# One ordered instruction region, four weighting buffers, paired weight sums, and SBUF pools moved to multiples of 512 bytes, in a fused linear-attention and expert kernel

## The chip, the cores and the metric

The kernel runs on one core of a Trainium2 chip. The metric is the device time of one execution in microseconds (us); lower is better. The granted clock of TensorE (PE) is given as a share of its full 2.4 GHz.

## The reference

Three stages follow each other; all data is float32.

```python
# 1: linear attention with a decaying state, batch 2, 8 heads, 768 steps, head size 48
cur = einsum('bhd,bhe->bhde', u * k_t, v_t)
y_t = einsum('bhd,bhde->bhe', r_t, state + cur)
state = w_t[..., None] * state + einsum('bhd,bhe->bhde', k_t, v_t)
# 2: x is y as 1536 tokens x 384; w_in 384 x 2048, w_out 2048 x 384
h = x @ w_in
x = where(h > 0, h, exp(min(h, 0)) - 1) @ w_out
# 3: four experts, w1[e] 384 x 1024, w2[e] 1024 x 384; p are normalised domain_probs
for e in range(4):
    out += p[:, e:e+1] * (maximum(x @ w1[e], 0) @ w2[e])
```

## The kernel before

Every 128x128 by 128x512 product is done in float32r with both operands split into a high and a low part: three matmuls (`PASSES`: high x high, high x low, low x high) accumulate in one PSUM bank. Splitting costs a copy on ScalarE (ACT) for the high part and a subtraction on VectorE (DVE) or GpSimd (POOL) for the low part, of weights and of activations alike.

The work runs in this order. The attention works on 12 chunks of 128 steps. The feed-forward stage has 48 steps (`step`): `h` multiplies tokens with `w_in` (L355, 9 matmuls), `e` and `el` make the activation and its low part, `z` multiplies with `w_out` (L375, 9 matmuls), `dr` adds a finished block into `x2` and splits it again. Its weights come in 32 pieces (`wl` load, `wa`, `wb`, `wc` convert). A hand-written list, `ORDER`, gives the sequence of attention and feed-forward tokens. A `|` in it (its place is `cut`) marks where the attention's memory is given up. What lies in front of it is one ordered region, what follows is a second one.

The expert stage (`experts`) is a third ordered region. It makes a list of events, each with a key, and issues them in order of key. The keys count the groups of three matmuls on PE: `row` has 36 groups `plain` (the first product of two units, L553), then `product` (L525) and `second` (L575) in turn, about five to six. The first product of the other 14 units is done for blocks of 2x3 weights and 3x3 tokens at once by a scheme of 15 products instead of 18. For it, sums of weight blocks are made on POOL (`sum_blocks`, L444, 11 of 128x128 for each unit, list `SUMS`) and sums of tokens on DVE (`TOKENS`, L505). `taken` (L537) adds the finished products into `terms` on DVE, `hidden_hi` (L565) and `hidden_lo` (L568) apply the maximum and split, `second` is the product with `w2`. After it `weighted` (L584, DVE) multiplies by the token's share into a `scaled` buffer, and `added` (L589, POOL) adds that to `x2`. `shares` (L478 to L486) makes the shares from `dp`, `load_share` spreads them. `load_blocks` (L440) and `load_second` (L462) load weights from the queue of SyncE (SP).

Events with negative keys belong in front of the first matmul of the stage: `shares` has -200, the loads of the first units have -95, -85 and -39, the weight sums of the first summed unit lie between -14 and -2.

Two regions are ordered each within itself. How the instructions of the third region stand between those of the second is decided when the program is built, not by the keys.

On-chip memory (SBUF) is handed out to pools from both ends, tile after tile, padded to 32 bytes. From the left, 2,176 bytes are taken (a 2,048-byte scratch area and four padded constants), then the pool `const` takes 704 bytes, then come `x` (49,152 bytes), `x2`, and the pools of the second and third stage, all in sizes that are multiples of 512. So each tile from `x` on begins 320 bytes past a multiple of 512: `x`, `w` of the feed-forward stage, `hl`, `w2s`. From the right, the top is 229,344; `xb` takes 12,288 bytes there and the others (`blocks`, `sums`, `raw2`) follow in multiples of 512, so each begins 480 bytes past one. The weights of `plain` and `product` are `sums` (480), those of `second` are `w2s` (320); the tokens that they stream are `x` (320), `xb` (480) and `hl` (320).

Of the kernel before, what the change touches and what calls it, by code (L numbers as in the profile page):

```python
# [9 lines left out]
F32 = mybir.dt.float32  # L10
F32R = mybir.dt.float32r
# [3 lines left out]
ALU = mybir.AluOpType  # L15
PSUM = bass.MemoryType.PSUM

P = 128
C = 128
NCH = 12  # L20
# [10 lines left out]
PASSES = ((0, 0), (0, 1), (1, 0))  # L31
WARM = 3
TERMS = 18

# [10 lines left out]
LOADED = [(0, 0), (1, 0), (0, 1), (1, 2), (0, 2), (1, 1)]  # L47
W0, W3, W1, W5, W2, W4 = range(5, 11)
SLOT = {11: 0, 0: 1, 8: 2, 9: 3, 14: 4, 7: W0, 2: W3, 3: W2, 6: W4, 4: 11, 10: 12, 13: 13, 5: 14, 12: 15, 1: 16}
SUMS = [(SLOT[0], W1, "-", W4), (SLOT[13], W1, "-", W0), (SLOT[4], SLOT[13], "-", W4), (SLOT[5], W5, "-", W3),  # L50
        (SLOT[10], SLOT[5], "-", W2), (SLOT[12], SLOT[13], "-", SLOT[5]), (SLOT[1], SLOT[10], "+", W0),
        (SLOT[11], SLOT[4], "+", W3), (SLOT[9], W2, "-", W5), (SLOT[8], W5, "-", W4), (SLOT[14], W2, "-", W1)]
PLACE = dict(zip(TURNS, [9, 10, 11, 12, 13, 14, 0, 3, 6, 1, 4, 7, 2, 5, 8]))

TOKENS = [("q", (1, 1), (2, 1)), (0, "q", (0, 1)), (6, (1, 2), None), (3, (2, 2), None), (4, 0, (1, 2)), (7, 4, (0, 2)),
# [5 lines left out]
ORDER = """  # L61
# [27 lines left out]
def kernel_body(ctx, tc, wkr, vv, uu, w_in, w_out, w1, w2, dp, out):  # L89
    nc = tc.nc  # L90
    const = ctx.enter_context(tc.tile_pool(name="const", bufs=1))
# [3 lines left out]
    pools = {}  # L95
# [9 lines left out]
    m1 = ExitStack()  # L105
# [11 lines left out]
    warm = bank()  # L117
    for _ in range(WARM):
        nc.tensor.matmul(warm, lhsT=first1[:, 0:P], rhs=first1[:, 0:512], start=True, stop=True)
    ones = const.tile([P, 1], F32, name="ones")  # L120
    nc.gpsimd.memset(ones, 1.0)
    ident = const.tile([P, P], F32, name="ident")
    make_identity(nc, ident)
# [271 lines left out]
    def do(order):  # L395
        for token in order:
            name, n, e = re.fullmatch(r"([a-z]+)(\d+)([ADMPS]?)", token).groups()
            kind = step if name in ("h", "e", "el", "z", "dr") else piece if name in ("wl", "wa", "wb", "wc") else attn
            if (kind, n) not in work:
                work[kind, n] = kind(int(n))  # L400
            work[kind, n][name](*e)

    cut = ORDER.index("|")
# [6 lines left out]
    def early_pools(es):  # L410
        for name, bufs in (("xb", 1), ("blocks", 2), ("sums", 3), ("raw2", 2)):
            pools[name] = es.enter_context(tc.tile_pool(name=name, bufs=bufs, side="right"))

    def late_pools(es):
        for name, bufs in (("w2", 2), ("terms", TERMS), ("hl", 4), ("shares", 4), ("scaled", 2), ("guard", 1)):
            pools[name] = es.enter_context(tc.tile_pool(name=name, bufs=bufs))
        for name, bufs in (("chain", 5), ("second", 3)):
            pools[name] = es.enter_context(tc.tile_pool(name=name, bufs=bufs, space=PSUM))
        pools["rows"] = es.enter_context(tc.tile_pool(name="rows", bufs=1, space=bass.MemoryType.DRAM))

    def experts(guard=False):

        events = []

        def at(key, run, *args):
            events.append((key, len(events), run, args))

        xb = pools["xb"].tile([P, 3, 2, 512], F32R, name="xb")
        pairs = x.rearrange("q k (b n) s c -> q (k b) (n s c)", b=3)

        def tokens(r):
# [4 lines left out]
        blocks, split = {}, {}  # L436

        def load_blocks(u):
            blocks[u] = pools["blocks"].tile([P, 17, P], F32, tag="blocks", name="blocks")
            nc.sync.dma_start(blocks[u][:, 5:11].rearrange("q b c -> q (b c)"), w1[:, u])  # L440

        def sum_blocks(u, r, a, op, c):
            t = blocks[u]
            nc.gpsimd.tensor_tensor(t[:, r], t[:, a], t[:, c], ALU.subtract if op == "-" else ALU.add)  # L444

        def split_hi(u, part, first, n, i, m):
            if i == 0:
# [27 lines left out]
        rows = pools["rows"].tile([4, NT], F32, name="rows")  # L475
        prs = {}

        def shares():  # L478
            t = pools["raw2"].tile([P, 768], F32, tag="raw2", name="share")
            share, total = t[:NCH, 0:512].rearrange("n (e c) -> n e c", e=4), t[:NCH, 512:640]  # L480
            nc.sync.dma_start(share, dp)
            nc.vector.tensor_reduce(total, share.rearrange("n e c -> n c e"), mybir.AxisListType.X, ALU.add)
            nc.vector.tensor_scalar_add(total, total, 1e-9)
            nc.vector.reciprocal(total, total)
            nc.vector.tensor_tensor(share, share, total.unsqueeze(1).to_broadcast([NCH, 4, C]), ALU.mult)
            nc.sync.dma_start(rows.rearrange("e (n c) -> n e c", n=NCH), share)  # L486
# [74 lines left out]
        hls, sums = {}, {}  # L561
# [7 lines left out]

        def second(h, b, f, d):  # L570
            if f == 0:
                sums[d] = pools["second"].tile([P, 512], F32, tag="second", name="second")
            w = w2s[h].rearrange("p s (f d) -> p s f d", f=4)
            for i, (sa, sm) in enumerate(PASSES):
                nc.tensor.matmul(sums[d], lhsT=w[:, sa, f, d * P:(d + 1) * P], rhs=hls[4 * h + f, b][:, sm],  # L575
                                 start=f == i == 0, stop=f == 3 and i == 2)

        scaled = {}
# [29 lines left out]
            nc.vector.tensor_reduce(flag, n, mybir.AxisListType.X, ALU.max)  # L608


        seconds = [(h, b, f, d) for h in range(8) for b in range(3) for f in range(4) for d in range(3)]
        row = [("plain", f, b, j) for b in range(3) for f in range(4) for j in range(3)]
        done = 0
# [6 lines left out]
        place = {g: n for n, g in enumerate(row)}  # L620
        for n, (kind, *g) in enumerate(row):
# [5 lines left out]
            elif kind == "second":  # L627
# [4 lines left out]
                if f == 3:  # L632
                    at(n + 0.6, weighted, *g[:2], d)
                    if h:
                        at(n + 0.8, added, *g[:2], d)
        at(-200, shares)
        for e in range(4):
            for b in range(3):
                at(place["second", 2 * e, b, 0, 0] - 60, load_share, e, b)
        for u in range(16):  # L640
            n = place["product", u, 0] if u > 1 else -20 + 10 * u
            at(n - 75, load_blocks, u)
            if u < 2:
                for i in (0, 3):
                    at(n - 20 + i, split_hi, u, 0, 5, 6, i, 3)
                    at(n - 19 + i, split_lo, u, 0, 5, 6, i, 3)
                continue
            for i, s in enumerate(SUMS):
                at(n - 50 + 1.2 * i, sum_blocks, u, *s)
            for part, first, size, k in ((0, 9, 8, n - 34), (1, 0, 7, n - 14)):  # L650
                for i in (0, 4):
                    at(k + i, split_hi, u, part, first, size, i, min(4, size - i))
                    at(k + i + 1.4, split_lo, u, part, first, size, i, min(4, size - i))
        for h in range(8):
            n = place["second", h, 0, 0, 0]
            for m in range(2):
                at(n - 70 + m, load_second, h, m)
                for q in range(2):
                    at(n - 38 + 6 * m + 3 * q, second_hi, h, m, q)
                    at(n - 37 + 6 * m + 3 * q, second_lo, h, m, q)  # L660
        for i, t in enumerate(TOKENS):
            at(1.2 + 1.1 * i, sum_tokens, *t)
        for i, r in enumerate(TURNS):
# [14 lines left out]

    early, late = ExitStack(), ExitStack()
    early_pools(early)  # L680
    with tc.manual_schedule():
        do(ORDER[cut + 1:])
    m1.close()
    late_pools(late)
    experts(guard=True)
    late.close()
    early.close()

# [112 lines left out]
```

## Time and profile before

| | us |
|---|---|
| median of 3 runs | 698.1 (695.83 to 701.0) |
| the profiled execution | 697.27 |
| its span, first to last instruction | 695.5 |
| PE busy in the span | 652.5 |
| DVE, POOL, ACT busy | 493.0, 413.6, 305.6 |

Busy time of PE includes the tail of each matmul, which overlaps the next one; so PE's speed is read from the distance between the starts of two matmuls (the pitch), and from idle time in front of one.

### The profile page before, as it was taken

Reading aid. Unit: us, or ns where it says so; the run is one execution under the profiler, and the core shown is the slowest. Engines: PE = TensorE matmul, PEld = TensorE weight load, DVE = VectorE, ACT = ScalarE, POOL = GpSimd, SP = SyncE. Lnnn points to the kernel's source line nnn. Section 1 sums busy time; section 2 is a strip of 40 time slices with the busy share of each in tenths; the row PEclk is TensorE's granted clock in tenths of the full one; section 3 lists DMA queues with packets and bytes.
Section 4 is the critical chain, followed back from the end, with each engine's and each line's share of the span. In section 5 each row is a group of like instructions: output and inputs, shape, how many; then the busy total and the mean of one; then the engine's idle time right before and its main releaser. Section 6 shows DMA issues by size and latency. Waiting matters only on the chain.

```text
span 695.5 us, 9183 instructions
## 1 busy us (share of the span) xinstructions
PE 652.5 (94%) x3314; PEld 521.1 (75%) x3314; DVE 493.0 (71%) x686; ACT 305.6 (44%) x584; POOL 413.6 (59%) x415
## 2 busy tenths in 40 slices
PE   6778999889999999999999999999999999999994
PEld 4666778668888888786888868778688688788773
DVE  7989997728563642798675777876867777777764
ACT  2343645637565663648343524433443335233220
POOL 5898684565332451659643865876876777644241
PEclk9989999999999999999999999999999999999998
DMA  7655552322202100011102121021120122200012
GB/s 264 206 180 182 180 186 62 115 89 82 83 24 68 47 24 1 3 65 50 57 17 74 63 60 54 23 85 31 42 94 15 39 68 69 76 0 1 0 46 96
DMA packets 20971, 50.83 MB, mean 73 GB/s; under 512 B 2680, under 2 KB 3880, under 8 KB 20916
## 3 DMA queue, kind: packets, MB, share of 16 engines
q1 hardware_dynamic: 20772, 50.15, 23.1%
q8 instruction: 28, 0.46, 0.3%
q14 instruction: 27, 0.22, 0.1%
q10 hardware_dynamic: 144, 0.00, 0.0%
HBM read 46.58 MB, written 2.38 MB: 70 GB/s over the span
## 4 chain that ended last, share of the span: by engine, by line
PE 68%; DVE 12%; POOL 11%; issue 6%; DMA 2%; ACT 1%; SPq 0%; DVEq 0%; POOLq 0%; ACTq 0%
PE second L575 25%; PE bank L375 11%; PE bank L355 9%; PE chain_a L525 8%; PE chain_b L525 4%; PE chain_c L525 3%; PE chain_d L525 3%; DVE terms L505 2%; DVE hl L568 2%; DVE scaled L584 2%; POOL x L589 2%; POOL rd L141 2%; POOL kr L141 1%; PE chain_e L525 1%; POOL hl L144 1%
## 5 line engine op out<-in xcount | busy, mean ns | idle before, releaser
L575 PE MATMUL second<-hl,w2s 128*128 128x512 f32 x864 | 237.0, 396 | 2.7 <-DVE scaled L584 1.4
L575 PEld LDWEIGHTS second<-hl,w2s 128*128 128x128 f32 x864 | 161.8, 188 | 43.6 <-DVE scaled L584 3.6
L589 POOL TENSOR_TENSOR x<-scaled,x 128x512 f32<-128x512 f32 x60 | 81.3, 1375 | 96.3 <-DVE scaled L584 96.3
L375 PE MATMUL bank<-hl,w 128*128 128x512 f32 x432 | 106.1, 396 | 4.4 <-POOL hl L144 4.2
L355 PE MATMUL bank<-x,w 128*128 128x512 f32 x432 | 104.0, 392 | 0.2 <-DVE e L363 0.2
L144 POOL TENSOR_TENSOR sums<-blocks,sums 128x512 fp32r<-128x512 f32 (+1 forms) x60 | 79.4, 1331 | 37.5 <-ACT sums L148 34.2
L375 PEld LDWEIGHTS bank<-hl,w 128*128 128x128 f32 x432 | 81.2, 190 | 23.2 <-POOL hl L144 5.2
L568 DVE SCALAR_TENSOR_TENSOR hl<-terms,hl 128x512 fp32r<-128x512 f32 x96 | 90.2, 943 | 7.1 <-ACT hl L565 6.8
L355 PEld LDWEIGHTS bank<-x,w 128*128 128x128 f32 x432 | 80.9, 188 | 18.0 <-DVE e L363 0.6
L444 POOL TENSOR_TENSOR blocks<-blocks 128x128 f32<-128x128 f32 x154 | 86.1, 583 | 1.2
L525 PE MATMUL chain_a<-x,sums 128*128 128x512 f32 x210 | 61.2, 399 | 6.4 <-DVE terms L537 6.3
L363 DVE SCALAR_TENSOR_TENSOR e<-e,bank 128x512 f32<-128x512 f32 x48 | 32.4, 681 | 47.6 <-ACT e L359 43.3
L565 ACT ACTIVATE hl<-terms 128x512 fp32r<-128x512 f32 x96 | 58.1, 623 | 16.4 <-PE second L575 11.5
L144 POOL TENSOR_TENSOR hl<-e,hl 128x512 fp32r<-128x512 f32 x26 | 35.2, 1358 | 49.4 <-ACT hl L148 48.8
L537 DVE TENSOR_TENSOR terms<-terms,chain_a 128x512 f32<-128x512 f32 x42 | 28.7, 684 | 42.2 <-PE chain_a L525 42.2
L148 ACT ACTIVATE sums<-blocks 128x512 fp32r<-128x512 f32 (+1 forms) x60 | 35.6, 595 | 49.7 <-PE chain_b L525 30.2
L148 ACT ACTIVATE terms<-chain_b 128x512 f32<-128x512 f32 x28 | 16.8, 600 | 88.7 <-PE chain_b L525 88.7
L525 PEld LDWEIGHTS chain_a<-x,sums 128*128 128x128 f32 x210 | 39.1, 188 | 18.0 <-DVE terms L537 9.0
L584 DVE TENSOR_TENSOR scaled<-second,pr 128x512 f32<-128x512 f32 x63 | 43.1, 685 | 13.3 <-PE second L575 8.5
L148 ACT ACTIVATE hl<-e 128x512 fp32r<-128x512 f32 x48 | 30.1, 629 | 34.3 <-PE bank L375 23.9
L358 ACT ACTIVATE e<-bank 128x512 f32<-128x512 f32 x48 | 28.5, 593 | 33.0 <-POOL hl L144 15.6
L148 ACT ACTIVATE terms<-chain_a 128x512 f32<-128x512 f32 x28 | 16.7, 598 | 50.4 <-PE chain_a L525 50.4
(116 smaller groups left out, 998.2 us busy)
## 6 DMA issues: line engine op xcount, KB each, us to landing
kr<-in_wkr SPq DMA_DIRECT2D x12, 512.0 KB, 3.9
raw<-in_w_in SPq DMA_DIRECT2D x16, 384.0 KB, 3.4
raw<-in_w_out SPq DMA_DIRECT2D x16, 384.0 KB, 3.3
blocks<-in_w SPq DMA_DIRECT2D x16, 384.0 KB, 3.4
raw<-in_w SPq DMA_DIRECT2D x16, 384.0 KB, 4.5
v<-in_vv SPq DMA_DIRECT2D x12, 456.0 KB, 4.4
w<-in_wkr SPq DMA_DIRECT2D x12, 258.5 KB, 4.0
gw<-in_wkr SPq DMA_DIRECT2D x12, 258.0 KB, 2.9
```

The lines of the kernel that those rows point to most:

```text
L144: engines[e].tensor_tensor(o, a, b.bitcast(F32), ALU.subtract)
L148: nc.scalar.activation(out=o, in_=a, func=AF.Copy)
L355: nc.tensor.matmul(ph, lhsT=wi[:, sa, f, kk, :], rhs=x[:, kk, c0:c0 + nch, sm], start=(kk == 0 and i == 0), stop=(kk == 2 and i == 2))
L363: nc.vector.scalar_tensor_tensor(b["e"], b["e"], -1.0, b["ph"], ALU.add, ALU.max)
L375: nc.tensor.matmul(pxs[q, bl][d], lhsT=wo[:, sa, f, d * P:(d + 1) * P], rhs=b["t"][:, sm], start=(f == 0 and i == 0), stop=(f == 3 and i = ...
L444: nc.gpsimd.tensor_tensor(t[:, r], t[:, a], t[:, c], ALU.subtract if op == "-" else ALU.add)
L525: nc.tensor.matmul(banks[c], lhsT=weights(u, r, sa), rhs=tokens(r)[:, sm], start=r in HEADS and i == 0, stop=i == 2, skip_group_check=True)
L565: nc.scalar.activation(out=hls[f, b][:, 0], in_=results[f, b], func=AF.Relu)
L568: nc.vector.scalar_tensor_tensor(hls[f, b][:, 1], results[f, b], 0.0, hls[f, b][:, 0].bitcast(F32), ALU.max, ALU.subtract)
L575: nc.tensor.matmul(sums[d], lhsT=w[:, sa, f, d * P:(d + 1) * P], rhs=hls[4 * h + f, b][:, sm], start=f == i == 0, stop=f == 3 and i == 2)
L584: nc.vector.tensor_tensor(o, sums[d], prs[h // 2, b], ALU.mult)
L589: (nc.vector if last else nc.gpsimd).tensor_tensor(x2[:, d, s], scaled[d], x2[:, d, s], ALU.add)
```

## The change

Five edits. The tokens behind `|` and the events of the expert stage become one ordered region: the tokens get negative keys, counted backwards from the end in steps of 3 for each `h` and `z` (which have 3 groups each), and `switch`, which closes the feed-forward pools and opens the late ones, is an event with key 0. So the tokens begin at about -237, the load for the shares is at -250 and their arithmetic at -100; events that need the late pools get a key of at least 0. The `scaled` pool has four buffers instead of two. Weight sums are made in pairs: six POOL instructions for a unit instead of eleven, five of them on two blocks at a time. The second products of the last half expert's middle block (h 7, b 1) accumulate in banks of the pool `chain`. And padding moves the pools: `const` becomes 896 bytes (`ones` is cut out of a 49-column tile), so the left side begins at a multiple of 512; `xb` becomes 12,768 bytes, so the right side does.

```diff
+EDGE = 120
-SUMS = [(SLOT[0], W1, "-", W4), (SLOT[13], W1, "-", W0), (SLOT[4], SLOT[13], "-", W4), (SLOT[5], W5, "-", W3),
-        (SLOT[10], SLOT[5], "-", W2), (SLOT[12], SLOT[13], "-", SLOT[5]), (SLOT[1], SLOT[10], "+", W0),
-        (SLOT[11], SLOT[4], "+", W3), (SLOT[9], W2, "-", W5), (SLOT[8], W5, "-", W4), (SLOT[14], W2, "-", W1)]
+SUMS = [((SLOT[13], SLOT[5]), (W1, W5), "-", (W0, W3)), ((SLOT[4], SLOT[12]), (SLOT[13],) * 2, "-", (W4, SLOT[5])),
+        ((SLOT[9], SLOT[10]), (W2, SLOT[5]), "-", (W5, W2)), ((SLOT[11], SLOT[1]), (SLOT[4], SLOT[10]), "+", (W3, W0)),
+        ((SLOT[0], SLOT[8]), (W1, W5), "-", (W4, W4)), ((SLOT[14],), (W2,), "-", (W1,))]
-    ones = const.tile([P, 1], F32, name="ones")
+    ones = const.tile([P, 49], F32, name="ones")[:, 0:1]
+        pools["rows"] = es.enter_context(tc.tile_pool(name="rows", bufs=1, space=bass.MemoryType.DRAM))
-        for name, bufs in (("w2", 2), ("terms", TERMS), ("hl", 4), ("shares", 4), ("scaled", 2), ("guard", 1)):
+        for name, bufs in (("w2", 2), ("terms", TERMS), ("hl", 4), ("shares", 4), ("scaled", 4), ("guard", 1)):
-        xb = pools["xb"].tile([P, 3, 2, 512], F32R, name="xb")
+        xb = pools["xb"].tile([P, 3072 + EDGE], F32R, name="xb")[:, 0:3072].rearrange("q (r s c) -> q r s c", r=3, s=2)
+        def places(t, p):
+            if p[0] == p[-1]:
+                return t[:, p[0]:p[0] + 1].to_broadcast([P, len(p), P])
+            d = p[1] - p[0]
+            return t[:, p[0]:p[1] + (1 if d > 0 else -1):d]
         def sum_blocks(u, r, a, op, c):
-            t = blocks[u]
-            nc.gpsimd.tensor_tensor(t[:, r], t[:, a], t[:, c], ALU.subtract if op == "-" else ALU.add)
+            nc.gpsimd.tensor_tensor(*(places(blocks[u], p) for p in (r, a, c)), ALU.subtract if op == "-" else ALU.add)
+        def load_shares():
+            given["t"] = pools["raw2"].tile([P, 768], F32, tag="raw2", name="share")
+            nc.sync.dma_start(given["t"][:NCH, 0:512].rearrange("n (e c) -> n e c", e=4), dp)
...
-                sums[d] = pools["second"].tile([P, 512], F32, tag="second", name="second")
+                k = "chain" if h == 7 and b == 1 else "second"
+                sums[d] = pools[k].tile([P, 512], F32, tag=k, name=k)
...
+        n, keys = 0, []
+        for token in reversed(lead):
+            n -= 3 * (token[0] in "hz")
+            keys.append(n)
+        for token, n in zip(lead, reversed(keys)):
+            at(n, do, [token])
+        if switch:
+            at(0, switch)
...
-        at(-200, shares)
+        at(-250, load_shares)
+        at(-100, shares)
-                at(place["second", 2 * e, b, 0, 0] - 60, load_share, e, b)
+                at(max(0, place["second", 2 * e, b, 0, 0] - 60), load_share, e, b)
-                at(n - 50 + 1.2 * i, sum_blocks, u, *s)
+                at(n - 50 + 2 * i, sum_blocks, u, *s)
-                    at(n - 38 + 6 * m + 3 * q, second_hi, h, m, q)
-                    at(n - 37 + 6 * m + 3 * q, second_lo, h, m, q)
+                    at(max(0, n - 38 + 6 * m + 3 * q), second_hi, h, m, q)
+                    at(max(0, n - 37 + 6 * m + 3 * q), second_lo, h, m, q)
...
-    with tc.manual_schedule():
-        do(ORDER[cut + 1:])
-    m1.close()
-    late_pools(late)
-    experts(guard=True)
+    def switch():
+        m1.close()
+        late_pools(late)
+    experts(guard=True, lead=ORDER[cut + 1:], switch=switch)
```

## Rows read from the trace of the kernel before

**Rows 1.** The page's first parts: engine busy times, and PE's granted clock by slice.
```profile
PE 652.5 (94%) x3314; PEld 521.1 (75%) x3314; DVE 493.0 (71%) x686; ACT 305.6 (44%) x584; POOL 413.6 (59%) x415
...
PEclk9989999999999999999999999999999999999998
```

**Rows 2.** Busy time by stretch; columns PE, PEld, DVE, ACT, POOL, granted clock, DMA.
```profile
118.00:293.00 175.00, 170.45 (x740) 139.15 (x739) 96.37 (x153) 99.97 (x178) 77.31 (x71) 0.99 0.19 55
...
290.00:330.00 40.00, 37.60 (x151) 28.99 (x150) 34.86 (x37) 25.16 (x48) 28.80 (x25) 0.96 0.14 48
330.00:658.00 328.00, 320.37 (x1366) 254.64 (x1364) 235.95 (x337) 122.05 (x229) 207.17 (x237) 1.00 0.15 47
658.00:696.00 38.00, 25.77 (x108) 19.32 (x107) 20.54 (x28) 5.09 (x9) 12.21 (x8) 0.92 0.17 65
```

**Rows 3.** PE in order of time in the feed-forward stage: start, length, count.
```profile
181.17 4.24 PE L355 MATMUL bank<-x,w 128*128 128x512 f32 x18
185.25 1.07 PE L375 MATMUL bank<-hl,w 128*128 128x512 f32 x4
```

**Rows 4.** The same in the plain products of the expert stage.
```profile
297.70 5.53 PE L553 MATMUL chain_p<-x,sums 128*128 128x512 f32 x23
```

**Rows 5.** The chain that ended last, 340 to 350 us: start, length, what, count.
```profile
339.84 0.70 PE chain_a L525 x3
...
349.60 0.47 PE second L575 x2
```

**Rows 6.** PE in order of time just after the first second products.
```profile
325.24 1.49 PE L575 MATMUL second<-hl,w2s 128*128 128x512 f32 x3
...
327.80 0.41 PE L575 MATMUL second<-hl,w2s 128*128 128x512 f32 x1
```

**Rows 7.** Busy time and granted clock in 325 to 327 us, columns as in group 2.
```profile
325.00:327.00 2.00, 2.00 (x7) 1.54 (x6) 1.34 (x3) 2.00 (x5) 2.00 (x3) 0.50 0.00 0
```

**Rows 8.** Busy time in 447 to 455 us, columns as in group 2.
```profile
447.00:455.00 8.00, 6.73 (x28) 4.73 (x26) 7.79 (x11) 1.30 (x3) 5.62 (x7) 1.00 0.01 3
```

**Rows 9.** POOL in order of time, 132 to 147 us.
```profile
140.10 5.18 POOL L444 TENSOR_TENSOR blocks<-blocks 128x128 f32<-128x128 f32 x11
145.24 1.26 POOL L144 TENSOR_TENSOR hl<-e,hl 128x512 fp32r<-128x512 f32 x1
```

**Rows 10.** PE in order of time, 133 to 152 us; in brackets the idle time ahead.
```profile
137.92 2.11 PE L375 MATMUL bank<-hl,w 128*128 128x512 f32 x8 [1.96 <-POOL hl L144]
...
146.55 3.49 PE L375 MATMUL bank<-hl,w 128*128 128x512 f32 x8 [2.22 <-POOL hl L144]
149.84 2.46 PE L355 MATMUL bank<-x,w 128*128 128x512 f32 x9
```

**Rows 11.** SP's queue in order of time, 118 to 140 us.
```profile
126.75 0.33 SPq L486 DMA_DIRECT2D rows<-share  x1
129.53 0.38 SPq L175 DMA_DIRECT2D raw<-in_w_out  x1
```

**Rows 12.** DVE in order of time, 448 to 456 us.
```profile
450.98 0.69 DVE L584 TENSOR_TENSOR scaled<-second,pr 128x512 f32<-128x512 f32 x1 [0.21 <-POOL x L589]
...
452.19 1.81 DVE L568 SCALAR_TENSOR_TENSOR hl<-terms,hl 128x512 fp32r<-128x512 f32 x1
```

**Rows 13.** PE's waits: for whom, us in total, times, longest.
```profile
PE chain_a L525 <- DVE terms L537: 6.3, 5, 1.3
...
PE second L575 <- DVE scaled L584: 1.4, 3, 0.8
PE chain_b L525 <- DVE terms L537: 1.3, 5, 0.3
```

**Rows 14.** POOL's groups by shape: busy us, mean ns of one, idle us ahead.
```profile
L444 POOL TENSOR_TENSOR blocks<-blocks 128x128 f32<-128x128 f32 x154 | 86.1, 583 | 1.2
...
L144 POOL TENSOR_TENSOR sums<-blocks,sums 128x384 fp32r<-128x384 f32 x18 | 20.1, 1120 | 3.2 <-DMA blocks<-in_w 3.2
L141 POOL TENSOR_TENSOR rd<-kr,a 128x512 f32<-128x512 f32 x11 | 18.0, 1633 | 5.3 <-DVE a L254 2.1 <-DVE raw L181 2.0 <-PE bank L327 1.2
```

## The prediction before the run

> **What bounds the kernel now.** I read the page's busy times first, then busy time by stretch, then PE in order of time, and last the waits. PE is busy 652.5 of 695.5 us and its granted clock is full in nearly every slice [rows 1]. From 118 to 293 us it has 170.5 of 175 busy, from 330 to 658 us 320.4 of 328 [rows 2]. There the time is the number of matmuls times their pitch, plus a few gaps. In between, from 290 to 330 us, DVE has 34.9 of 40 us and PE waits for token sums: DVE bounds that stretch [rows 2].
>
> So the pitch is the first thing to look at, and it isn't one number. In the feed-forward stage 18 matmuls start in 185.25 - 181.17 = 4.08 us, 226.7 ns each [rows 3]; a single one's record is 4.24 less 17 pitches, 0.39 us. In the plain products it is (5.53 - 0.39) / 22 = 233.6 ns [rows 4]. Where `product` and `second` take turns, 42 matmuls pass from 339.84 to 349.60, 232.4 ns each [rows 5]. All of these are matmuls of 512 columns at the full clock. Just after a gap of PE six matmuls take 327.80 - 325.24 = 2.56 us, 426.7 ns each [rows 6], and the granted clock there is 0.50, the 1.2 GHz level [rows 7]: exactly 512 columns at that clock. At 2.4 GHz the same would be 213.3. So at the full clock something other than the columns adds 13.3 ns in the feed-forward stage and 20 in the plain products, and at half the clock it is hidden.
>
> What differs between these two places is where the weights lie: 320 bytes past a multiple of 512 (`w`), 480 past it (`sums`). The streamed tokens (`x`, 320) are the same, with the same strides. 13.3 to 20 is 2 to 3, and 320 to 480 is 2 to 3 as well, also when one counts from the last multiple of 128 (64 and 96). A straight line through the two points meets zero excess at offset zero. Two points are few, but this is the reading that I bet on.
>
> **The change part by part.** The sum is made against the profiled execution's 697.3 us, 0.8 under the median of the runs.
>
> *Alignment.* No row shows a weight tile on a multiple of 512, so its pitch lies between 213.3 (the columns alone) and today's 226.7, and above that if two equal offsets get in each other's way. I take 213.3, where the line through the two rows ends. Feed-forward: 740 matmuls between 118 and 293 us [rows 2] x 13.4 ns = 9.9 us (in front of 118 the attention sets the pace, and I count nothing). From 290 to 330 us nothing, because DVE bounds it. From 330 to 658 us: 1366 matmuls [rows 2] x 19.1 ns = 26.1 us, less the spots where DVE is full, 7.79 of 8 us [rows 8], at the end of each of six half experts: 6 x 28 matmuls x 19.1 ns = 3.2 us don't count there. 22.9 us remain. In the tail 108 matmuls [rows 2], most of them at 226.7 already by the same way of counting: 108 x 13.4 = 1.5 us. Together 34.3 us.
>
> The Trainium skill (TensorE: Matmul & The Clock Gate, Back-to-back issue gap) gives N / 2.4 + 2.5 ns for the warm gap, 215.8 for 512 columns. The trace shows 226.7 at best, so this chip's kernel doesn't reach it before the change. With 215.8 as the aligned pitch the sum below would be about 5 us smaller and the time near 657.
>
> *One ordered region.* Today the work for the experts is done early, around 119 to 145 us, in front of the feed-forward work that PE needs. On POOL eleven weight sums take 5.18 us from 140.10, and the low part `hl` that PE waits for comes behind them at 145.24 [rows 9]. PE idles 1.96 us at 137.92 and 2.22 at 146.55, and after the second gap eight matmuls take 3.29 us instead of 1.81, the clock having fallen [rows 10]. On SP the store of the shares waits for DVE until 126.75, and the load of `w_out` behind it goes at 129.53 [rows 11]. After the change the shares come at -100 (some 67 us before the stage's end), the splits of the first units at -40 to -26, the sums at -14 to -4. These gaps go: 2.0 + 2.2 + 1.5 + 0.3 for the restarts = 6.0 us. The work itself doesn't go; it is put between the `e`, `el` and `z` of the late feed-forward stage, where POOL is busy for 77 of 175 us and DVE for 96 [rows 2]. The queues are in order, so each such block can hold back one `hl`: the eleven sums as six take about 5 us on POOL, in six places. The bounds are nothing and the whole 6 us again on each of the two engines, 12; I take 1.5, since the pieces are spread and the engines are half idle. On SP, the share's load now waits at the region's head for memory of the attention; behind it are the next `wl` loads. Net 4.5 us. The order behind key 0 hardly changes, so the stretch at 290 to 330 us stays as it is.
>
> *Four `scaled` buffers.* At the end of each half expert DVE's third `weighted` waits 0.21 us for POOL's `added`, and the `hidden_lo` behind it takes 1.81 us [rows 12] where others of its kind take 0.7, as it meets POOL's three additions. Then PE waits for `terms` of DVE, 6.3 us and 1.3 us in five places each [rows 13]. With four buffers the 0.21 us surely goes and part of the 1.1. Bounds: 0.2 x 6 = 1.2 us and the whole wait, 7.6 plus restarts, about 10. I take 0.8 a place, 4.8 us: DVE's own work is what is late next, full as it is.
>
> *Chain banks for h 7, b 1.* In the tail PE waits for a bank until DVE has multiplied, three times, 1.4 us [rows 13]. Two of the three places go, with their restarts and the wait behind them for the guard's small matmul: 2.0 us. The first place, at the start of h 7, stays.
>
> *Paired sums.* POOL's sum of 128 columns takes 583 ns, its operations on 384 take 1120 [rows 14]; a pair of 256 lies between, I take 0.85 us. A unit then costs 5 x 0.85 + 0.58 = 4.8 us instead of 6.4. POOL isn't the bound (207 of 328 us [rows 2]), so it is costed at nothing; POOL's slack is its cover.
>
> Sum: 34.3 + 4.5 + 4.8 + 2.0 = 45.6; 697.3 - 45.6 = 651.7 us.
>
> **The rivals.** *Only unequal offsets cost.* The feed-forward stage has tokens and weights both at 320 and the lowest pitch; the others mix 320 and 480. If the difference matters and not the offset itself, everything goes to 226.7: 1366 x 5.7 ns = 7.8 us, with the other edits 7.8 + 4.5 + 4.0 + 2.0 = 18.3, 679 us. For it: products that stream `xb` (480 with weights at 480) weren't slower than the others. Against it: the excess is not zero where both are equal.
>
> *The offset doesn't matter at all*, and the pitches differ because of the order of operands or the mix of stages. Then 697.3 - 11.3 = 686 us. The Trainium skill (SBUF — State Buffer, Specifications) knows lines of 16 bytes, and both 320 and 480 are multiples of 16; its section Who interferes with whom says that PE never waits on anyone. By that rule this rival is the case. The trace has three pitches for one shape of matmul, which neither section explains.
>
> *Paired sums run slowly on POOL.* One operand's blocks are 9 or 16 blocks apart, one goes backwards, two are repeated. If a pair cost more than about 2.5 us, POOL's share of a unit (207 us less 86 for sums, over 14 units, plus 13) would pass the 22 us that PE needs and POOL would set the pace. At 3 us each it is 8.6 + 15.6 = 24.2 us a unit, 2 to 3 us too much, 14 times: with the rest gained or not, some 705 to 715 us. Against it: `rd`, whose second operand is four runs in strides, takes 1633 ns for 512 columns [rows 14].
>
> **How the numbers follow.** The forecast, the pitch near 213 everywhere: 0.46, 644 to 664 us by the bounds of the gaps, the delayed `hl` and a floor some ns higher. Unequal offsets: 0.25, 672 to 684. No effect: 0.20, 680 to 692. Slow pairs, or equal offsets that collide: 0.09. The range 644 to 688 leaves out the last and half of the tail of the third. The three runs before lie within 0.4% of the median, so about 1% is what can be told from no change, 691 to 705 us. Faster by more: the first two and three quarters of the third, 0.86; within: 0.07; slower: 0.07.
>
> **What would show it.** In the profile after: 18 matmuls in about 3.85 us in the feed-forward stage, six in 1.28 to 1.30 us where `product` and `second` take turns. If it is 4.08 and 1.36, unequal offsets were the cause; if 4.08 and 1.39, nothing was. No gap of PE between 130 and 160 us; new ones, if any, after POOL's or DVE's work near 225 or 275 to 290 us. No wait of `scaled` for `added`. PE's gaps at the end of each half expert remain, shorter, and DVE near full around them. The prediction is wrong above all if the line through two points is no line.

## The result and the profile after

The changed kernel takes 681.1 us (median of 4 runs, 679.2 to 681.6), the kernel before 697.4 (695.8 to 701.0): ratio 0.975, 95% interval 0.971 to 0.980. So it is 16.3 us faster, where 45.6 had been forecast; the time lies in the range given, close to the 679 us of the rival *only unequal offsets cost*. The profiled execution took 681.25 us, with a span of 679.4.

First the page's busy times and granted clock, to be held against [rows 1]:

```profile
PE 643.0 (95%) x3314; PEld 523.8 (77%) x3314; DVE 493.6 (73%) x686; ACT 305.7 (45%) x584; POOL 403.2 (59%) x345
...
PEclk7689999999999999999899999999999999999997
```

PE has the same 3314 matmuls as before in 9.5 us less, and DVE is as busy as it was. The clock is lower in the first slices, in the attention stage. Next PE in order of time in the feed-forward stage:

```profile
176.16 4.24 PE L357 MATMUL bank<-x,w 128*128 128x512 f32 x18
180.24 4.24 PE L377 MATMUL bank<-hl,w 128*128 128x512 f32 x18
```

18 matmuls start in 4.08 us, 226.7 ns each, to the digit what [rows 3] had. Nothing has changed there, though `x` and `w` now lie on multiples of 512. Now busy time by stretch, columns as in group 2:

```profile
118.00:290.00 172.00, 171.50 (x761) 140.25 (x757) 97.67 (x157) 101.89 (x182) 75.99 (x65) 1.00 0.21 61
290.00:330.00 40.00, 33.60 (x134) 26.16 (x135) 36.81 (x35) 24.22 (x47) 32.57 (x25) 0.96 0.17 56
330.00:658.00 328.00, 324.11 (x1422) 265.34 (x1422) 246.09 (x351) 125.83 (x235) 204.14 (x179) 1.00 0.15 47
```

Set beside [rows 2]: in the same 328 us behind 330, PE does 1422 matmuls where it did 1366. From 290 to 330 it does fewer, 134 for 151, with less busy time (33.6 us for 37.6), while DVE (36.8 for 34.9) and POOL (32.6 for 28.8) have more. Part of that is only that the stage now begins at 290.8 us and not at 294.8. Counted from its first plain product, the 120th matmul behind it starts after 35.6 us where it took 31.7; so that stretch did become worse. For the steps themselves (the prediction's pitch, from the start of one matmul to that of the next) I take 60 us in which PE never pauses, 340 to 400; the first row is the kernel before, the second the changed one:

```profile
340.00:400.00 60.00, 60.00 (x260) 48.44 (x259) 41.85 (x64) 25.44 (x49) 33.74 (x44) 1.00 0.17 51
```
```profile
340.00:400.00 60.00, 60.00 (x266) 49.69 (x265) 44.79 (x67) 25.32 (x48) 31.51 (x31) 1.00 0.17 51
```

266 matmuls for 260. Over the 1,225 and 1,294 steps of under 240 ns between 340 and 640 us, the mean goes from 232.5 to 226.9 ns; the three places that the prediction looked at at full clock now show one number. Six steps are 1.36 us, and with 4.08 in the feed-forward stage that is the sign that the prediction had set for its rival. PE's waits behind 330 us:

```profile
PE chain_a L536 <- DVE terms L548: 1.6, 5, 0.3
PE chain_n L619 <- DVE ends L617: 1.4, 1, 1.4
PE second L587 <- DVE scaled L596: 0.9, 1, 0.9
```

Against [rows 13], the wait at the end of each half expert is 0.3 us where it was 1.3, that of `chain_b` is gone, and of the three waits for `scaled` in the tail one is left. And the stretch that became worse, PE in order of time (in brackets the idle time ahead):

```profile
310.77 2.37 PE L564 MATMUL chain_p<-x,sums 128*128 128x512 f32 x9 [1.29 <-ACT terms L150]
...
320.75 0.49 PE L587 MATMUL second<-hl,w2s 128*128 128x512 f32 x1 [1.43 <-ACT hl L576]
323.31 0.73 PE L587 MATMUL second<-hl,w2s 128*128 128x512 f32 x2 [2.07 <-DVE hl L579]
...
325.08 1.48 PE L587 MATMUL second<-hl,w2s 128*128 128x512 f32 x3
```

The wait for DVE's first `hl` is 2.07 us; before, the longest wait at this place was 0.7 us. The three matmuls at 325.08 start 427 ns apart: half the clock again, as in [rows 6, 7], after the pause.

Which steps were the long ones can be read from the kernel before, and speaks against the simplest form of the rival. Its `second` matmuls have weights and tokens both at 320. In turn with the products they take 232.4 ns from one to the next (489 steps between 340 and 640 us); in the tail, where more than a dozen of them follow each other without a pause, 226.7. Products with both sides at 480 (`xb`, `sums`) take 232.3. So it isn't a matmul's own two tiles that make its step long: where PE takes turns between the two sides, every step is longer.

To compare runs stage by stage I took four moments out of each trace: the end of the last attention matmul, the start of the first plain product, the start of the first second product, and the end of the last matmul.

| run | attention ends | feed-forward stage | plain stage | rest |
|---|---|---|---|---|
| before | 116.7 | 178.1 | 27.6 | 363.4 |
| changed | 118.7 | 172.0 | 30.0 | 348.7 |
| e1 not aligned | 117.4 | 173.0 | 30.0 | 354.7 |
| e2 aligned only | 120.6 | 176.6 | 27.6 | 354.9 |
| e3 both at 320 | 117.1 | 172.7 | 30.0 | 348.6 |
| e4 0 and 256 | 119.8 | 172.0 | 30.0 | 348.6 |
| e5 two regions | 118.0 | 175.8 | 28.4 | 348.5 |
| e6 two `scaled` | 118.4 | 172.4 | 30.0 | 356.6 |
| e7 single sums | 118.9 | 172.6 | 29.6 | 345.8 |
| e8 bank undone | 117.4 | 172.3 | 30.0 | 350.2 |
| e9 464 columns | 117.5 | 166.2 | 30.1 | 334.2 |
| e10 0 and 64 | 117.6 | 171.8 | 30.0 | 353.0 |
| e11 0 and 128 | 117.1 | 171.8 | 30.0 | 354.4 |
| e12 low part on POOL | 117.8 | 172.8 | 30.4 | 345.7 |

The 16.3 us are -6.1 in the feed-forward stage, +2.4 in the plain stage, -14.7 behind it and +2.1 in front. The last I don't put down to the change: the first column lies between 116.7 and 120.6 in these runs, and e4, e10 and e11, which differ in `EDGE` alone, have 119.8, 117.6 and 117.1. The last column has a part of that kind too. After the pause at 323 us, 7 steps of 427 ns follow in the changed kernel, 11 or 12 in e1, e6, e8 and e11, and none in e7; four or five more are 0.8 to 1.0 us, and with one trace of each run I can't tell whether the edit made them.

### The profile page after: what moved, and what is told of

It is laid out like the page before. It is cut to its first block, busy times and chain, and to the rows that moved or that the text cites. A ratio compares the mean times of both kernels' runs of the same rounds, so it can differ in the third digit from the quotient of the medians.

```text
span 679.4 us, 9111 instructions
## 1 busy us (share of the span) xinstructions
PE 643.0 (95%) x3314; PEld 523.8 (77%) x3314; DVE 493.6 (73%) x686; ACT 305.7 (45%) x584; POOL 403.2 (59%) x345
## 4 chain that ended last, share of the span: by engine, by line
PE 76%; DVE 12%; POOL 4%; issue 3%; DMA 2%; ACT 2%; SPq 1%; DVEq 0%; POOLq 0%; ACTq 0%
PE second L587 24%; PE bank L357 13%; PE bank L377 12%; PE chain_a L536 8%; PE chain_b L536 5%; PE chain_c L536 3%; DVE terms L516 3%; PE chain_d L536 2%; PE bank L278 2%; PE bank L285 2%; DVE scaled L596 2%; DVE terms L548 1%; PE chain_e L536 1%; PE bank L329 1%; DVE w2s L146 1%
## 5 line engine op out<-in xcount | busy, mean ns | idle before, releaser
L587 PE MATMUL second<-hl,w2s 128*128 128x512 f32 x828 | 223.4, 391 | 4.4 <-DVE hl L579 2.1
L587 PEld LDWEIGHTS second<-hl,w2s 128*128 128x128 f32 x828 | 155.8, 188 | 38.1 <-DVE hl L579 2.4
L601 POOL TENSOR_TENSOR x<-scaled,x 128x512 f32<-128x512 f32 x60 | 84.9, 1437 | 96.1 <-DVE scaled L596 96.1
L146 POOL TENSOR_TENSOR sums<-blocks,sums 128x512 fp32r<-128x512 f32 (+1 forms) x60 | 83.3, 1397 | 36.4 <-ACT sums L150 36.4
L377 PE MATMUL bank<-hl,w 128*128 128x512 f32 x432 | 104.1, 391 | 0.1
L579 DVE SCALAR_TENSOR_TENSOR hl<-terms,hl 128x512 fp32r<-128x512 f32 x96 | 87.6, 916 | 8.0 <-ACT hl L576 7.9
L451 POOL TENSOR_TENSOR blocks<-blocks 128x256 f32<-128x256 f32 x84 | 69.4, 837 | 1.1
L576 ACT ACTIVATE hl<-terms 128x512 fp32r<-128x512 f32 x96 | 58.1, 624 | 16.3 <-PE chain L587 6.1
L150 ACT ACTIVATE hl<-e 128x512 fp32r<-128x512 f32 x48 | 30.1, 629 | 36.4 <-PE bank L377 24.8
L596 DVE TENSOR_TENSOR scaled<-second,pr 128x512 f32<-128x512 f32 x60 | 39.3, 680 | 5.8 <-PE second L587 5.8
L360 ACT ACTIVATE e<-bank 128x512 f32<-128x512 f32 x48 | 28.4, 592 | 26.3 <-PE bank L357 13.4
```

The source lines that it names most:

```text
L146: engines[e].tensor_tensor(o, a, b.bitcast(F32), ALU.subtract)
L150: nc.scalar.activation(out=o, in_=a, func=AF.Copy)
L377: nc.tensor.matmul(pxs[q, bl][d], lhsT=wo[:, sa, f, d * P:(d + 1) * P], rhs=b["t"][:, sm], start=(f == 0 and i == 0), stop=(f == 3 and i = ...
L451: nc.gpsimd.tensor_tensor(*(places(blocks[u], p) for p in (r, a, c)), ALU.subtract if op == "-" else ALU.add)
L576: nc.scalar.activation(out=hls[f, b][:, 0], in_=results[f, b], func=AF.Relu)
L579: nc.vector.scalar_tensor_tensor(hls[f, b][:, 1], results[f, b], 0.0, hls[f, b][:, 0].bitcast(F32), ALU.max, ALU.subtract)
```

## The experiments

The theory after the first look: unequal places of the two sides that PE reads cost about 6 ns a matmul, and with equal places 226.7 ns is what there is, wherever they lie. The rivals: the multiple of 512 itself counts; or alignment brought nothing and other edits moved the pitch; or it brought the 34 us and DVE took them back.

**The pads alone, and all but the pads.** e1 is the changed kernel with

```
-EDGE = 120
+EDGE = 0
-ones = const.tile([P, 49], F32, name="ones")[:, 0:1]
+ones = const.tile([P, 1], F32, name="ones")
```

and e2 the kernel before with these two lines the other way round, and the line of the change that makes `xb` longer by `EDGE`.

> The changed kernel with its two pads taken out: the tiles on the left lie 320 bytes past a multiple of 512 again, xb, sums and raw2 480 past one. Theory (only unequal offsets cost, some 6 ns a matmul): the pitch is 226.7 ns in the feed-forward stage and about 232.5 to 233.5 behind 330 us; 1422 matmuls x 5.8 ns = 8 us longer than the changed kernel, about 689 us. Rival 1 (the pads cost nothing and bring nothing, the pitch fell through another edit): 681 us and 226.7 ns everywhere. Rival 2 (the pads brought much more, which was lost again elsewhere): 695 or more.

> The kernel before with the two pads alone. Theory: 226.7 ns everywhere, 1366 matmuls x 5.8 ns less = 8 us shorter than the kernel before, about 689 us, all of it behind 330 us, and the feed-forward stage as long as before. Rival (the pads do nothing by themselves): 697 us. The forecast's own reading (the pitch falls to 213.3) is already gone: it would give 663.

e1: 686.2 us, ratio to before 0.983 (0.981 to 0.985). e2: 691.0, ratio 0.990 (0.988 to 0.992). The alignment is worth 5.2 us taken out and 6.8 put in alone. The steps agree (232.4 ns in e1, in the feed-forward stage 226.9 as ever). In e2 the part behind the plain stage is 8.5 us shorter, as expected; the first column hides some of it in the total. In e1 the 8 us don't all come: PE's pause at the end of each half expert is shorter, 0.30 us from start to start where the changed kernel has 0.71, in five places. A slower PE gives DVE time to catch up, and takes back some of its own price.

**Where equal, where not.** e3 has everything 320 bytes past a multiple of 512 (`EDGE = 40`, `ones` of one column); e4, e10 and e11 have the left side at 0 and `xb`, `sums`, `raw2` at 256, 64 and 128 (`EDGE` 56, 104 and 88).

> The changed kernel with all the pools that TensorE reads 320 bytes past a multiple of 512, on the left and on the right: equal offsets, but not zero. Theory (equality alone counts): 226.7 ns everywhere, 681 us, the same as the changed kernel. Rival (the multiple of 512 itself counts): the pitch behind 330 us is 229 to 234 ns and the time 685 to 690 us.

> The changed kernel with the left side on a multiple of 512 and xb, sums and raw2 256 bytes past one: an inequality of 256, where the kernel before had one of 160. Theory, if any inequality costs: 232 to 234 ns behind 330 us, about 689 us. If the cost grows with the inequality: 235 ns or more, 692 or more. If only the place within 64, 128 or 256 bytes counts: 226.7 ns and 681 us.

> The changed kernel with the left side on a multiple of 512 and xb, sums and raw2 64 bytes past one. If the place within 64 bytes counts (160 cost something, 256 nothing): 226.7 ns, 681 us. If the place within 128 or 256 bytes counts: 230 ns or more behind 330 us and 685 to 690 us.

> The changed kernel with the left side on a multiple of 512 and xb, sums and raw2 128 bytes past one. If the place within 64 or 128 bytes counts: 226.7 ns, 681 us. If the place within 256 bytes counts: 230 ns or more behind 330 us and 685 to 690 us.

e3: 679.9 us (ratio 0.975, 0.972 to 0.977). e4: 681.3 (0.977, 0.974 to 0.979). e10: 685.0 (0.983, 0.981 to 0.986). e11: 683.8 (0.982, 0.979 to 0.985). The unpaused 60 us of e3, e4, e10 and e11, in this order:

```profile
340.00:400.00 60.00, 60.00 (x267) 49.67 (x265) 44.83 (x67) 25.34 (x48) 31.50 (x30) 1.00 0.17 51
```
```profile
340.00:400.00 60.00, 60.00 (x266) 49.69 (x265) 44.81 (x67) 26.06 (x50) 31.87 (x30) 1.00 0.17 51
```
```profile
340.00:400.00 60.00, 60.00 (x260) 48.60 (x259) 44.56 (x65) 25.32 (x48) 29.81 (x29) 1.00 0.17 51
```
```profile
340.00:400.00 60.00, 60.00 (x260) 48.64 (x259) 44.49 (x65) 25.32 (x48) 29.76 (x30) 1.00 0.17 51
```

The mean steps between 340 and 640 us are 226.9, 226.8, 231.7 and 231.9 ns (of those under 250 ns, as e10 and e11 have some above 240). A difference of 0 or 256 bytes costs nothing, one of 64, 128 or 160 (before) costs 4.8 to 5.6 ns, far from in proportion to the difference. The multiple of 512 is of no use in itself: e3 lies nowhere near one.

The pads move whole sides, with tiles of the other engines on them; that these could be the cause is a rival of its own. The feed-forward stage speaks against it. There PE reads the left side alone, while POOL, DVE and ACT already work on `blocks` and `sums` on the right: in the kernel before, e1, e10 and e11 the some 30 steps beside such an operation take 226.7 to 227.5 ns, the others 226.8 to 226.9. That speaks for what PE itself reads; which pairs of its reads meet isn't shown.

**The other edits, one undone at a time.** e5 is the kernel before with pads, four buffers, the banks and the paired sums, that is, without the one region. The others are the changed kernel with one edit undone:

```
e6:  -("scaled", 4)   +("scaled", 2)
e7:  -nc.gpsimd.tensor_tensor(*(places(blocks[u], p) for p in (r, a, c)), ...)
     +nc.gpsimd.tensor_tensor(t[:, r], t[:, a], t[:, c], ...)     (eleven sums, 1.2 apart)
e8:  -k = "chain" if h == 7 and b == 1 else "second"   +k = "second"
```

> The changed kernel with all but the one region: the experts' early work stands in a region of its own behind the feed-forward order, as before; pads, four weighting buffers, the two chain banks and the paired sums stay. The prediction's own term: 4.5 us longer than the changed kernel, 685.6. By the two traces: the gaps around 137 and 146 us come back (some 6 us), but the stretch from 290 to 330 us takes the later arrival without a loss, so 0 to 2 us longer, 681 to 683. Rival (the region is worth its 6 us in full): 687.

> The changed kernel with two weighting buffers in place of four. The prediction's term: 4.8 us longer, 686. By the two traces: the gap at the end of each half expert goes from about 0.7 back to about 2 us in five or six places, 7 to 8 us longer, 688 to 689. Rival (the gap shrank because of the other edits): 681 to 683.

> The changed kernel with the eleven weight sums one at a time again. The prediction's term: nothing, 681, as POOL has slack. Rival (POOL's time counts between 290 and 330 us and beside the end of each half expert, where its operations and DVE's lengthen each other): 1.6 us more of POOL's time a unit, 683 to 688 us.

> The changed kernel with the last expert's second block in the three banks of its own kind again, not in chain banks. The prediction's term: 2.0 us longer, 683, all of it behind 640 us. Rival (another wait of the tail hides it): 681.

e5: 683.3 us (0.980, 0.977 to 0.983). e6: 687.7 (0.985, 0.982 to 0.988). e7: 678.9 (0.973, 0.970 to 0.975). e8: 681.8 (0.977, 0.974 to 0.980). PE at the end of the first half expert, in e6 and then in the changed kernel (in brackets the pause ahead):

```profile
405.93 0.96 PE L536 MATMUL chain_a<-x,sums 128*128 128x512 f32 x3 [1.26 <-DVE terms L548]
```
```profile
403.56 0.73 PE L536 MATMUL chain_a<-x,sums 128*128 128x512 f32 x2 [0.31 <-DVE terms L548]
```

Only e6 is clearly apart from the changed kernel by its interval. For e5, e7 and e8 the stages say more than the totals: e5 loses 3.8 us in the feed-forward stage (the gap of 2.0 us for POOL's `hl` is back, with eight matmuls at half the clock behind it; the second gap is not) and has 1.6 less in the plain stage. e7 gains 2.9 in the rest (e12 below, which also has single sums, 3.0). The end of the stretch from 290 to 330 us is the place: counted from the first plain product, e7 is 3.2 us ahead at 330 us and 3.4 at the end. Below are e7's rows, then its DVE there:

```profile
290.00:330.00 40.00, 35.60 (x148) 27.14 (x148) 35.82 (x37) 24.59 (x47) 33.02 (x32) 1.00 0.16 52
330.00:658.00 328.00, 324.07 (x1422) 265.55 (x1422) 241.97 (x351) 126.52 (x236) 216.71 (x241) 1.00 0.15 47
```
```profile
315.19 0.95 DVE L511 TENSOR_TENSOR terms<-terms 128x512 f32<-128x512 f32 x1
316.06 0.95 DVE L519 SCALAR_TENSOR_TENSOR x<-terms,x 128x512 fp32r<-128x512 f32 x1
316.93 1.81 DVE L511 TENSOR_TENSOR terms<-terms,x 128x512 f32<-128x512 f32 x2
```

and the same four operations on DVE in the changed kernel:

```profile
314.08 1.23 DVE L516 TENSOR_TENSOR terms<-terms 128x512 f32<-128x512 f32 x1
315.23 1.22 DVE L524 SCALAR_TENSOR_TENSOR x<-terms,x 128x512 fp32r<-128x512 f32 x1
316.38 2.93 DVE L516 TENSOR_TENSOR terms<-terms,x 128x512 f32<-128x512 f32 x2
```

Beside them POOL does, first in the changed kernel, then in e7:

```profile
313.57 3.48 POOL L451 TENSOR_TENSOR blocks<-blocks 128x256 f32<-128x256 f32 x3
317.02 1.74 POOL L146 TENSOR_TENSOR sums<-blocks,sums 128x512 fp32r<-128x512 f32 x1
```
```profile
314.68 3.52 POOL L446 TENSOR_TENSOR blocks<-blocks 128x128 f32<-128x128 f32 x4
318.16 1.73 POOL L146 TENSOR_TENSOR sums<-blocks,sums 128x512 fp32r<-128x512 f32 x1
```

All the sums on POOL, first two at a time in the changed kernel (14 of the 84 are the single eleventh), then one at a time in e7:

```profile
L451 POOL TENSOR_TENSOR blocks<-blocks 128x256 f32<-128x256 f32 x84 | 69.4, 837 | 1.1
```
```profile
L446 POOL TENSOR_TENSOR blocks<-blocks 128x128 f32<-128x128 f32 x154 | 85.7, 579 | 1.1
```

With pairs POOL has less work, 69.4 us for 85.7, but DVE beside it takes longer. Here each of DVE's operations lasts about as long as the one of POOL beside it: 1.22 us beside a pair (1.07 to 1.19), 0.95 beside a single sum (0.79 to 0.91), 1.78 beside a split of `sums` (1.74). So DVE gets as many operations done as POOL does, and longer ones on POOL slow it down; the 2.93 us are one operation beside a pair and one beside the split. The first `hl` comes later, PE pauses 2.07 us for it instead of 0.70, and its clock falls, which it doesn't in e7 (granted 0.96 for 1.00). Behind 330 us DVE also takes longer, 246.1 us instead of 242.0 for 351 operations, but that costs PE only the 0.2 us above. The Trainium skill (SBUF — State Buffer, Who interferes with whom) says that a DVE instruction with two inputs in SBUF gets in the way of a GpSimd instruction that reads there; the token sums are of that kind, and the durations above agree.

**A lower pitch by force.** e9 cuts the second and third matmul of each three to 464 columns:

```
+m = 464 if i else 512
-nc.tensor.matmul(banks[c], lhsT=..., rhs=tokens(r)[:, sm],
+nc.tensor.matmul(banks[c][:, 0:m], lhsT=..., rhs=tokens(r)[:, sm, 0:m],
...
```

> The changed kernel, but the second and third matmul of each group of three cover 464 of the 512 columns (58 in each half of... no other work is left out): the last columns lack these two partial products. It puts a lower pitch in by force, (226.7 + 2 x 206) / 3 = 213 ns on average, which the prediction had expected from the alignment, and asks what it would have been worth. If PE's pitch is all that counts, as the prediction's sum had it: 740 + 1422 matmuls x 13.7 ns = 29 us shorter than the changed kernel, 652 us. Rival (DVE sets the stretch from 290 to 330 us and the end of each half expert, so that what the feed-forward stage gains is lost there): the 10 us of the feed-forward stage go, and part of the other 19; 660 to 668 us. It also tells whether the 13.4 ns above the columns' own time are the same for fewer columns: 193.3 + 13.4 = 206.7 ns if they are, 205.4 if they shrink with the columns.

(The words "58 in each half of..." in it are a slip and mean nothing.) 659.9 us, ratio 0.946 (0.944 to 0.948): 21.2 us less than the changed kernel. The steps weren't as assumed. Behind 330 us the step from 512 to 464 took 226.4 ns, 464 to 464 206.4, 464 to the next 512 214.5, a mean of 215.8 and not 213; in the feed-forward stage the mean was 217.5. So what was put in is 740 x 9.4 + 1422 x 11.1 = 22.7 us, and 21.2 came out (5.8 in the feed-forward stage and 14.5 in the rest). PE's steps reach the end almost in full, and DVE would not have taken the gain back: that rival falls for the 11 ns a step that were put in, while the prediction's 13.4 to 19.1 weren't reached. (The plain stage stayed at 30.1 us, as the prediction had it.)

**What the 13.4 ns are.** e13 and e15 leave 512 columns but load only 64 or 32 of the 128 weight columns for the second matmul of each three (`lhsT=...[:, 0:m]` into `...[0:m]`); e16 is e9 with 448 columns.

> The changed kernel, but the second matmul of each group of three loads only 64 of its 128 weight columns (its product for the other 64 output rows is left out); all stream 512 columns. Theory (the 13.4 ns above the columns' own 213.3 are what the load of the next weights takes away from the stream, by its size): the step between two matmuls of which the second has the short weights falls from 226.7 to about 220 ns, the others stay. Rival (13.4 ns is a fixed price of a matmul, whatever it loads): 226.7 ns for all three. Rival (the short ones run in another way altogether): a step below 213.

> The same with 32 of the 128 weight columns in the second matmul of each three. By the size of the load: the step in front of it falls to about 216.7 ns. Fixed price: 226.7 ns.

> The run with 464 columns again with 448 (the second and third matmul of each three leave out the last 64 columns): 464 columns of 4 bytes are 7.25 times 256 bytes, 448 are 7 times. With 464 two of the three steps between matmuls had 13.1 ns above the columns' time and one had 21.2. Theory (steps are even where everything that PE reads is in whole 256 bytes): all three have 13 ns, that is 226.7, 200.0 and 200.0 ns. Rival (a change of the length by itself costs something, or the price is no matter of whole 256 bytes): one or more of the steps has 17 to 21 ns again, 204 to 208.

Each was run once: 684.6, 687.1 and 656.3 us. All three theories fall. Shorter loads made the steps longer: in e13 228.8 ns in front of the short one and 230.5 and 230.0 for the others, in e15 229.5, 233.0 and 230.9. With 448 columns (186.7 ns) the steps were 231.3, 203.3 and 204.1, that is 17 to 18 ns above the columns each, 17.3 on average where 464 had 15.8. (The rival of e16's expectation, 17 to 21 ns again, is met.) So it is neither the size of the load nor a fixed price nor a matter of whole 256 bytes in the stream. All that the runs say is that every departure from the regular case (512 columns, 128 weight columns, places equal within 256 bytes) had more than its 13.4 ns on average. What these consist of stays open.

**Relief for the plain stage.** e12 has single sums and makes the low parts of the first expert's `w2s` on POOL:

```
-sub("D", w2s[h][:, 1, s], ...)
+sub("P" if h == 0 else "D", w2s[h][:, 1, s], ...)
```

> The changed kernel with single weight sums, as in the run before that was 2 us shorter, and with the four low parts of the first expert's w2s made by POOL in place of DVE. Theory (DVE sets the stretch from 290 to 330 us): DVE loses four operations of 1.1 to 1.6 us each there, POOL does them while it waits for token sums; PE's gaps behind 305 us shrink by 2 to 4 us and the time is 675 to 677. Rival (POOL or ACT is next in line at once): 678 to 680.

678.3 us (0.974, 0.972 to 0.977), the same as e7: the rival. PE now waits 2.6 us once for ACT's `terms`, and POOL is nearly full:

```profile
290.00:330.00 40.00, 35.63 (x145) 28.23 (x146) 35.01 (x32) 23.78 (x46) 38.63 (x35) 0.96 0.15 51
```

Against e7 DVE's busy time in that stretch falls by 0.8 us and POOL's grows by 5.6, so moving the work gained nothing. e7 and e12 are the fastest kernels that do all the work, 2 to 3 us under the changed one, with intervals that still overlap its own.

## Why the prediction was wrong, point by point

*Alignment, 34.3 us.* This is the step that failed: "A straight line through the two points meets zero excess at offset zero." It measured 5.2 to 6.8. The two points, the feed-forward stage and the plain products, do differ in where the weights lie, but what counts is whether the tiles that PE reads in one stretch lie equally within 256 bytes, and in the feed-forward stage they did already. Both readings fit two points, but the third place of the prediction didn't fit the line: `second` has its weights at 320 like the feed-forward stage, and took 232.4 ns in turn with the products and 226.7 alone in the tail. These steps were in the trace of the kernel before: the prediction took its mean over both kinds of matmul, and itself put the tail at 226.7. The prediction named the right reading as a rival (0.25) and put 0.46 on the line because an excess was left where the places were equal. That excess is there, 13.4 ns at every equal place (e3, e4), and no alignment removes it. So the feed-forward term of 9.9 us and the 1.5 of the tail are nothing, and of the 26.1 behind 330 us only the rival's part remains: 1422 x 5.6 ns = 8 us by the steps, less what the shorter pauses of a slower PE return.

That the total lies 2 us from the rival's 679 is partly luck. Its terms were 7.8, 4.5, 4.0 and 2.0 us, with nothing for the pairs; undone one at a time they were worth 5.2, 2.2, 6.6, 0.7 and -2.2.

*The offset doesn't matter* (rival, 0.20) falls with e1 against e3. The Trainium skill (SBUF — State Buffer, Who interferes with whom) gives PE two independent read ports that it shares with no other engine. The prediction took from that section that places can't matter; here the measurement decides, as 64 bytes between the sides (e10) lengthen the steps from 226.9 to 231.7 ns.

*One ordered region, 4.5 us net.* The gaps at 137 and 146 us went, and the feed-forward stage is 6.1 us shorter, as the 6.0 had it; but by e5 only 3.8 of these are the region's, as the second gap was gone there too, without it. New gaps of some 0.3 us each at 243, 264 and 283 us are the small change expected. But "the stretch at 290 to 330 us stays as it is" was wrong: the plain stage became 2.4 us longer, 1.6 of them by the region (e5). Net about 2 us by e5.

*Four `scaled` buffers, 4.8 us.* The mechanism was right, the size low: 6.6 us in e6. At the end of a half expert in e6, with two buffers, the wait for `added` and the long `hl` of [rows 12] are there; in the changed kernel, shown second, the wait is gone and the same `hl` takes 0.86 us instead of 1.81:

```profile
448.46 0.69 DVE L596 TENSOR_TENSOR scaled<-second,pr 128x512 f32<-128x512 f32 x1 [0.22 <-POOL x L601]
449.67 1.80 DVE L579 SCALAR_TENSOR_TENSOR hl<-terms,hl 128x512 fp32r<-128x512 f32 x1
```
```profile
445.80 0.68 DVE L596 TENSOR_TENSOR scaled<-second,pr 128x512 f32<-128x512 f32 x1
447.00 0.86 DVE L579 SCALAR_TENSOR_TENSOR hl<-terms,hl 128x512 fp32r<-128x512 f32 x1
```

PE's pauses, with the slower first steps behind them, were about 2.0 us before, 1.9 in e6 and 0.6 in the changed kernel, in five places: 1.2 to 1.3 each by e6, where 0.8 had been taken. The sixth place gives 0.6 us.

*Chain banks, 2.0 us.* The wrong edit was credited here. Of the three waits for `scaled` only one is left, but in e8, with the banks undone, the other two have also shrunk, to steps of 404 ns; what shrank them isn't shown. The banks take these away, and the wait for the guard's matmul is 1.4 us with them, 1.1 without (0.6 before). What is left is 0.3 us in the tail; the rest of e8's 1.5 in the last column lies between 318 and 330 us, with its 12 steps at half the clock.

*Paired sums, nothing.* The duration was about right (0.85 taken; 0.905 measured for a pair, 0.84 with the single ones). That POOL's slack would cover it was not: the pairs lengthen DVE's operations beside them. By the totals they cost about 2 us, with intervals that overlap; by the last column of e7 and e12, about 3.

Undone one at a time the five edits make 5.2 + 2.2 + 6.6 + 0.7 - 2.2 = 12.5 of the 16.3 us. They overlap, the pauses of PE and the alignment above all (e1), so the parts needn't make the sum.

## What to carry to other kernels

Where one shape of matmul shows several pitches, write down the place of *each* operand beside each pitch before fitting one of them: here the difference of the two sides, taken modulo 256 bytes, explained what the place of one tile seemed to, and one small pad decides it. Look also at the same instruction in two surroundings: `second` alone and `second` in turn with another matmul told the two readings apart without any run. A residual that doesn't vanish where the suspected cause is absent speaks against an extrapolation to zero; its case should be priced as the floor. And fewer but longer operations on an engine with slack aren't free, if those of the full engine last as long as the ones beside them.

## What was unexpected of the hardware

- TensorE's step for 512 columns at 2.4 GHz was 226.7 to 226.9 ns wherever both sides that it read lay equally within 256 bytes, and 231.7 to 232.5 at differences of 64, 128 and 160, for matmuls with both of their own tiles on one side too.
- Loading fewer weight columns for every third matmul made the steps longer (229.8 ns on average with 64, 231.1 with 32), although the load itself fell from 188 to 134 and 108 ns.
- Shorter streams kept more than the 13.4 ns on average: 215.8 ns for a mean of 480 columns (200.0 by the columns), 212.9 for a mean of 469 (195.6).
- Between 313 and 322 us each operation of DVE on two SBUF tiles lasted about as long as POOL's beside it: 0.95 us beside 0.79 to 0.91, 1.22 beside 1.07 to 1.19, 1.78 beside 1.74.
